# Order of the first loads and casts, zero matmuls ahead of the hash products, and GpSimd output splits in the last pair of an LSH attention with two MLPs

## The chip, the cores and the metric

The kernel runs on one core of a Trainium2 chip. The time is the device time of one execution in microseconds (us); of several executions the median counts. The engines are TensorE (matmuls and transposes), VectorE, ScalarE, GpSimd and SyncE; rows of the profile call them PE (and PEld for its weight loads), DVE, ACT, POOL and SP. Each runs its own instructions in the order of the program and waits at semaphores for the others. DMA transfers are issued by SyncE, ScalarE or GpSimd.

## The reference

Attention within hash buckets, and then two MLPs on the result:

```python
def _attn_ref(q, k, v, proj):                  # q, k, v: (2, 8, 768, 64); proj: (64, 6)
    q_bits = (np.einsum('bhsd,dk->bhsk', q, proj) > 0).astype(np.int64)
    k_bits = (np.einsum('bhsd,dk->bhsk', k, proj) > 0).astype(np.int64)
    powers = 2 ** np.arange(n_bits)
    q_bucket = np.sum(q_bits * powers, axis=-1)
    k_bucket = np.sum(k_bits * powers, axis=-1)
    mask = q_bucket[:, :, :, None] == k_bucket[:, :, None, :]
    scores = scale * np.matmul(q, k.transpose(0, 1, 3, 2))
    scores = np.where(mask, scores, -1000000000.0)
    scores = scores - np.max(scores, axis=-1, keepdims=True)
    attn = np.exp(scores)
    attn = attn / (np.sum(attn, axis=-1, keepdims=True) + 1e-09)
    return np.matmul(attn, v)

def _moe_ref(x, w_gate, w_val, w_out):         # x: (1536, 512), inner width 1536
    gate = 1.0 / (1.0 + np.exp(-(x @ w_gate)))
    return gate * (x @ w_val) @ w_out

def _moe2_ref(x, w_in, w_out):                 # inner width 2048
    h = x @ w_in
    g = np.where(h >= 1, h, np.where(h <= -1, 0.0, (h + 1) ** 2 / 4))
    return g @ w_out
```

The three weights of the first MLP and the two of the second come as 64-bit floats; the attention's tensors are 32-bit.

## The kernel before

**Attention.** Heads are worked in eight pairs, four for each of the two batches. A pair is 12 units: a head (two) times a block of 128 queries (six). For a unit, `QK` makes 128x768 scores with eight or fewer matmuls in two banks, `MAX` (VectorE, line 304) the negated row maximum, `EXP` (ScalarE, line 308) the exponentials P and their row sums. `Flip` turns P: `T` transposes it on TensorE into a pt tile (two buffers, line 330), `HI` (ScalarE, line 339) and `LO` (VectorE, line 342) write its high and low half in 16 bits into PT. The products with v (`pv`, line 381) add up in a tile O; `evac` (VectorE, line 388) multiplies it by the reciprocal row sums and writes the attention output xr. The reciprocals are spread over 64 columns by GpSimd (`rb`, line 316), transposed on TensorE (r, line 499) and copied by ScalarE (rs).

**Operands.** All matmuls that need 32-bit accuracy work on a high half and a low remainder. `Prep` makes them for q and k of a pair: U is the high half and W the remainder; in a second role, H and N hold the one-hot rows of the hash buckets beside a head's values, so that the mask is part of the product. Two heads lie in the upper and lower 64 partitions, so halves have to be moved between partitions by DMA (line 274; for the first pair `first_moves`, line 245, which fills B, N and H from U, and `swap`, line 258, which writes W's half over the U half that was moved away). The hash: `z` (line 218) multiplies U and W by the projection in pz, `bits` (ScalarE, line 221) takes signs into bt, `xp` (line 227) multiplies bt by the code table, and `Hot` and `Hot_k` (lines 232 and 261) turn that into one-hot rows.

For the first pair U is made by ScalarE and W by VectorE (`UW`, lines 199 and 200); for the later pairs both by GpSimd (`scale`, `top`, `rest`). v is scaled by its largest magnitude and split by GpSimd (`split_v`: the reduction vm on VectorE, a row vrow through two small DMAs, then three GpSimd steps).

**MLPs.** The attention output is split the same way: `split` makes the high half on ScalarE (line 140) and the remainder on VectorE (line 141), four tiles x_0 to x_3 for each batch. `gv` makes the first chunk of gate and value products for batch 0 in two halves of 24 matmuls, still among the attention's work; a program-wide loop over further chunks, `out1` and `mlp2` follow. The 64-bit weights are brought to 32 bits with ScalarE and VectorE steps (`conv_w`, lines 94 to 104); those of the first chunk are made during the first pair by a generator `first_weights`, called as `fw`.

**The order.** All of attention is written under a manual schedule: engines run what the program says in that order. The start (`constants`, loads, hash of pair 0) is written out by hand. After it each step has a due time in units, from the table `AT` or a number beside `at(...)`; the steps are sorted by due time, and this is the order on each engine. `UP` is 12, so a pair's steps are 12 later than those of the pair ahead of it. SyncE's DMAs stand in the same order in one queue. The attention outputs of batch 0 are split at 1.5, 4.5, 7.5 and 10.5 of the last pair, those of batch 1 from 13 on, and `gv(0)` stands at 12.6.

## Time and profile before

| | us |
|---|---|
| median of three runs | 841.71 (840.47 to 841.99) |
| profiled execution | 837.76 |
| its span, first to last instruction | 836.0 |

| engine | busy us of the span | instructions |
|---|---|---|
| PE | 802.6 (96%) | 5072 |
| PEld | 734.8 (88%) | 5072 |
| DVE | 557.4 (67%) | 982 |
| ACT | 461.9 (55%) | 877 |
| POOL | 102.3 (12%) | 92 |

TensorE is busy through nearly all of the span, so the whole is read by stretches: the first 44 us fill the pipeline, the pairs in the middle run back to back, the last pair and the first gate products lie between 216 and 272 us, and the MLPs follow to the end. In the profile's 40 slices of 20.9 us, TensorE shows 3 tenths in the first slice, 7 in the second, 8 in the twelfth and thirteenth, 7 in the last, and else 9.

### The profile page before, as it was taken

How to read it: one execution, taken by the hardware profiler on the slowest of the kernel's cores; microseconds unless marked ns; L12 is line 12 of the kernel's file. 1: busy time of each engine (PE TensorE's matmuls, PEld its weight loads, DVE VectorE, ACT ScalarE, POOL GpSimd, SP SyncE). 2: the span in 40 equal slices, each digit the busy share in tenths (PEclk: the TensorE clock that was granted, in tenths of full speed). 3: DMA queues.
4: the chain of work that ended last, by engine and by line, in shares of the span. 5: the costliest groups of instructions: out<-in, count | busy, mean ns of one | idle time of the engine just before them, and what ended most of it. 6: DMA issues, size and time to landing. Idle time of an engine off the chain costs nothing.

```text
span 836.0 us, 13001 instructions
## 1 busy us (share of the span) xinstructions
PE 802.6 (96%) x5072; PEld 734.8 (88%) x5072; DVE 557.4 (67%) x982; ACT 461.9 (55%) x877; POOL 102.3 (12%) x92
## 2 busy tenths in 40 slices
PE   3799999999988999999999999999999999999997
PEld 2688888888766999999999999999989898989996
DVE  5898889889984845434588777999943435444443
ACT  3788888888874423222333345557654555555453
POOL 5254345435020000000000000000000000000000
PEclk9899999999999999999999999999999999999999
DMA  7444443453200521221146330543300001000001
GB/s 210 109 100 114 124 113 89 114 141 69 58 1 1 183 70 51 82 70 51 51 156 188 110 102 0 176 152 118 111 1 1 0 1 76 1 1 1 0 1 77
DMA packets 39486, 64.22 MB, mean 77 GB/s; under 512 B 5220, under 2 KB 27876, under 8 KB 39424
## 3 DMA queue, kind: packets, MB, share of 16 engines
q1 hardware_dynamic: 39168, 63.20, 26.0%
q8 instruction: 40, 0.66, 0.3%
q14 instruction: 22, 0.18, 0.1%
q0 software_dynamic: 112, 0.12, 0.1%
q10 hardware_dynamic: 144, 0.07, 0.0%
HBM read 45.27 MB, written 3.15 MB: 58 GB/s over the span
## 4 chain that ended last, share of the span: by engine, by line
PE 87%; DVE 6%; ACT 3%; DMA 2%; issue 1%; POOL 0%; DVEq 0%; ACTq 0%; SPq 0%; POOLq 0%
PE sc L296 7%; PE pt L330 7%; PE O L381 6%; PE p L127 5%; PE p L129 5%; PE p L128 5%; PE o L654 5%; PE o L655 5%; PE o L653 5%; PE pg L129 4%; PE pv L129 4%; PE pg L127 4%; PE pv L127 4%; PE pv L128 4%; PE pg L128 4%; PE y L127 3%
## 5 line engine op out<-in xcount | busy, mean ns | idle before, releaser
L342 DVE SCALAR_TENSOR_TENSOR PT<-pt,PT 128x512 f16<-128x512 f32 x144 | 96.2, 684 | 10.0 <-ACT PT L339 6.8
L339 ACT ACTIVATE PT<-pt 128x512 f16<-128x512 f32 x144 | 82.3, 597 | 24.9 <-PE pt L330 23.9
L304 DVE TENSOR_REDUCE st<-sc 128x1 f32<-128x768 f32 x96 | 90.7, 946 | 7.4 <-PE sc L296 7.4
L308 ACT ACTIVATE P<-sc,st 128x768 f32<-128x768 f32 x96 | 86.8, 904 | 11.6 <-DVE st L304 11.5
L330 PE MATMUL pt<-ident,P 128*128 128x128 f32 x576 | 83.5, 279 | 7.0 <-DVE PT L342 6.2
L127 PE MATMUL p<-yh,wh_i 128*128 128x384 f32 x256 | 86.0, 336 | 0.2 <-DVE yl L610 0.2
L129 PE MATMUL p<-yh,wl_i 128*128 128x384 f32 x256 | 85.9, 336 | 0.0
L128 PE MATMUL p<-yl,wh_i 128*128 128x384 f32 x256 | 85.7, 335 | 0.0
L330 PEld LDWEIGHTS pt<-ident,P 128*128 128x128 f32 x576 | 66.2, 142 | 21.4 <-DVE PT L342 15.0
L655 PE MATMUL o<-wh_o,gl 128*128 128x512 f32 x192 | 75.3, 392 | 0.0
L654 PE MATMUL o<-wl_o,gh 128*128 128x512 f32 x192 | 75.2, 392 | 0.0
L653 PE MATMUL o<-wh_o,gh 128*128 128x512 f32 x192 | 74.7, 389 | 0.0
L637 DVE SCALAR_TENSOR_TENSOR g<-p,t 128x384 f32<-128x384 f32 x64 | 35.4, 553 | 48.3 <-ACT t L635 48.3
L153 DVE SCALAR_TENSOR_TENSOR h<-sg,pv 128x384 f32<-128x384 f32 x48 | 26.4, 550 | 56.0 <-PE pv L129 56.0
L151 ACT ACTIVATE sg<-pg 128x384 f32<-128x384 f32 x48 | 23.4, 487 | 66.1 <-PE pg L129 65.8
L381 PE MATMUL O<-PT,vh 128*64 128x256 f16 x576 | 54.9, 278 | 2.6 <-DVE xr L388 2.6
L634 ACT ACTIVATE t<-p,cst 128x384 f32<-128x384 f32 x64 | 36.6, 572 | 36.8 <-PE p L129 36.8
L638 ACT ACTIVATE gh<-g 128x384 fp32r<-128x384 f32 x64 | 33.6, 525 | 41.8 <-DVE g L637 41.7
L639 DVE TENSOR_TENSOR gl<-g,gh 128x384 fp32r<-128x384 f32 x64 | 35.7, 557 | 31.5 <-ACT gh L638 31.5
L127 PEld LDWEIGHTS p<-yh,wh_i 128*128 128x128 f32 x256 | 48.1, 188 | 1.6 <-DVE yl L610 0.5
L128 PEld LDWEIGHTS p<-yl,wh_i 128*128 128x128 f32 x256 | 48.1, 188 | 1.1
L117 DVE TENSOR_TENSOR wl_o<-w_o,wh_o 128x512 fp32r<-128x512 f32 x56 | 38.5, 688 | 14.6 <-ACT wh_o L116 14.6
(256 smaller groups left out, 2009.9 us busy)
## 6 DMA issues: line engine op xcount, KB each, us to landing
wr_o<-in_moe_w_out_dram SPq DMA_DIRECT2D x28, 512.0 KB, 3.5
wr_i<-in_moe_w_in_dram SPq DMA_DIRECT2D x16, 512.0 KB, 3.8
wr_g<-in_moe_w_gate_dram SPq DMA_DIRECT2D x12, 512.0 KB, 3.8
wr_v<-in_moe_w_val_dram SPq DMA_DIRECT2D x12, 512.0 KB, 4.2
n<-in_qt_dram SPq DMA_DIRECT2D x8, 384.0 KB, 3.5
n<-in_kt_dram SPq DMA_DIRECT2D x8, 384.0 KB, 3.9
U<-W SPq DMA_DIRECT2D x16, 192.0 KB, 2.5
vr<-in_v_dram SPq DMA_DIRECT2D x8, 384.0 KB, 3.6
```

What stands on the lines that cost most here:

```text
L127: nc.tensor.matmul(ps, lhsT=wh, rhs=rh, start=first, stop=False)
L128: nc.tensor.matmul(ps, lhsT=wh, rhs=rl, start=False, stop=False)
L129: nc.tensor.matmul(ps, lhsT=wl, rhs=rh, start=False, stop=last)
L304: nc.vector.tensor_reduce(out=self.st[:, 0, self.c:self.c + 1], in_=self.sc[:, :, 0:HN], op=ALU.max, axis=AX.XY, negate=True)
L308: nc.scalar.activation(out=self.P, in_=self.sc[:, :, 0:HN], func=AF.Exp, bias=self.st[:, 0, self.c:self.c + 1], scale=1.0, accum_out=self. ...
L330: nc.tensor.transpose(self.ps[m][:, j, :], un[2 * self.n + e].P[:, a, c:c + 128], ident)
L339: nc.scalar.activation(out=self.part(0, m), in_=self.ps[m], func=AF.Copy, scale=PSCALE)
L342: nc.vector.scalar_tensor_tensor(out=self.part(1, m), in0=self.ps[m], scalar=PSCALE, in1=self.part(0, m), op0=ALU.mult, op1=ALU.subtract)
L381: nc.tensor.matmul(O_ps[r, 0:GN], lhsT=vv[m][:, e, i * D:(i + 1) * D], rhs=PT[:, l, e * NI + i, :], start=(s == 0), stop=(s == len(steps) ...
L653: nc.tensor.matmul(oacc[i], lhsT=gh[:, ts], rhs=wh, start=(fc == 0), stop=False)
L654: nc.tensor.matmul(oacc[i], lhsT=gh[:, ts], rhs=wl, start=False, stop=False)
L655: nc.tensor.matmul(oacc[i], lhsT=gl[:, ts], rhs=wh, start=False, stop=(fc == F2 - 1))
```

## The change

Five things are changed.

1. The projection's two loads are issued by ScalarE ahead of ident, where GpSimd issued them; the code table's load is GpSimd's first instruction, where it was the last of its constants. bt is zeroed by VectorE, ahead of pz.
2. The code table is cast by VectorE right behind pz, where the cast stood behind the B casts of the first pair. The first step of `first_weights` (ScalarE's w_abs) moves behind the one-hot rows of pair 0.
3. Twelve matmuls of bt by itself, when bt is all zeros, stand ahead of the hash products; they write a score bank that nothing reads.
4. For the first pair, the vm reduction of v and the four small steps on vrow stand later. For all others, the copies N<-U of the next pair are due right behind the GpSimd cast that makes U, and some due times of GpSimd steps have other numbers. The rb copy is a step of its own with the same due time.
5. `split_x` is made of two GpSimd instructions; batch 0's stand at 5.0, 6.7, 8.4 and 10.1 of the last pair, three of batch 1's behind the last reciprocals. The last split of batch 1 stays with ScalarE and VectorE and moves ahead of the second half of `gv`.

```diff
     def constants():
+        nc.scalar.dma_start(proj_sb[E], proj)
+        nc.scalar.dma_start(proj_sb[O], proj)
+        nc.gpsimd.dma_start(code_f, code_d)
+        nc.scalar.dma_start(ident, ident_d)
+        nc.vector.memset(bt, 0.0)
         nc.vector.memset(pz.bitcast(F32), 0.0)
         nc.gpsimd.memset(code, 0.0)
-        nc.gpsimd.memset(bt, 0.0)
...
-        nc.scalar.dma_start(ident, ident_d)
-        nc.gpsimd.dma_start(proj_sb[E], proj)
-        nc.gpsimd.dma_start(proj_sb[O], proj)
-        nc.gpsimd.dma_start(code_f, code_d)
...
+        nc.vector.tensor_copy(code[0:ZR], code_f)
...
             load_qk(*seq[1], nc.sync)
+            idle = sc_tile("idle")
+            for i in range(12):
+                nc.tensor.matmul(idle[:, 0, 0:HN], lhsT=bt[:, 0:128], rhs=bt, start=True, stop=True)
...
-            next(fw)
             p1.scale()
...
-            nc.vector.tensor_copy(code[0:ZR], code_f)
             pp.bits()
...
             pp.done()
+            next(fw)
...
+                "TOP": (-3.20, -1.20),
+                "RST": (-2.90, -0.90),
...
             def split_x(b, c):
-                X[b, c] = split(X[b, c], f"x{b}_{c}", qtile)
+                src, hi, lo = X[b, c], qtile(f"x{b}_{c}h"), qtile(f"x{b}_{c}l")
+                nc.gpsimd.tensor_copy(out=hi, in_=src)
+                nc.gpsimd.tensor_tensor(out=lo, in0=src, in1=f(hi), op=ALU.subtract)
+                X[b, c] = hi, lo
...
-                at("VR", 0, q - 1, split_v, b, p, 0)
-                at("VT", 0, q - 1, split_v, b, p, 1)
-                for h, d in ((2, 1.65), (3, 2.65), (4, 4.65)):
+                vs = [AT["VR"][0] - UP, AT["VT"][0] - UP, AT["V2"][0], AT["V3"][0], AT["V4"][0]]
+                if q == 0:
+                    vs[:2] = AT["MAX"][1] + 0.001, AT["MAX"][2] + 0.3
...
-                    at(-0.7 if q else -0.9, 0, q, on, q + 1, "copy", 0, 0)
-                    at(-0.65, 0, q, on, q + 1, "copy", 1, 0)
+                    at(AT["TOP"][0] + 0.001 if q else -0.9, 0, q, on, q + 1, "copy", 0, 0)
+                    at(AT["TOP"][1] + 0.001 if q else -0.65, 0, q, on, q + 1, "copy", 1, 0)
...
             for c in range(KC):
-                at(1.5 + 3 * c, 0, last, split_x, 0, c)
+                at(5.0 + 1.7 * c, 0, last, split_x, 0, c)
             for c in range(KC - 1):
-                at(UP + 1.0 + 0.7 * c, 0, last, split_x, 1, c)
-            at(UP + 0.6, 0, last, gv, 0)
+                at(AT["ST"][2] + 0.1 + 0.01 * c, 0, last, split_x, 1, c)
+            at(AT["T"][17] + 0.5, 0, last, gv, 0)
             for d, o, fn, args in sorted(prog, key=lambda x: x[:2]):
                 fn(*args)
+            X[1, KC - 1] = split(X[1, KC - 1], f"x1_{KC - 1}", qtile)
             gv(1)
-            split_x(1, KC - 1)
```

VectorE at the start of the program, before: W are the remainders of pair 0's q and k, B their moved copies, code the cast table, H and N one-hot rows, vm the reduction of v, st a row maximum.

```order
L200 SCALAR_TENSOR_TENSOR W_0_0_102<-n_0_0_76,U_0_0_101 128x768
L200 SCALAR_TENSOR_TENSOR W_0_0_106<-n_0_0_78,U_0_0_105 128x768
L253 CAST B_119<-W_0_0_102 64x768
L253 CAST B_123<-W_0_0_106 64x768
L450 CAST code<-code_f 56x512
L261 TENSOR_SCALAR H_0_0_107<-xp_0_0_162 64x768
L261 TENSOR_SCALAR N_0_0_108<-xp_0_0_162 64x768
L350 TENSOR_REDUCE vm_0_174<-vr_0_153 128x1
L304 TENSOR_REDUCE st_0_0_0_178<-sc_0_0_0_169 128x1
```

The cast of the table stands behind W and B, and vm ahead of the first maximum. The same place now (its line numbers are one higher, or one lower for vm):

```order
L75 CAST code<-code_f 56x512
L201 SCALAR_TENSOR_TENSOR W_0_0_116<-n_0_0_76,U_0_0_115 128x768
L201 SCALAR_TENSOR_TENSOR W_0_0_120<-n_0_0_78,U_0_0_119 128x768
L254 CAST B_133<-W_0_0_116 64x768
L254 CAST B_137<-W_0_0_120 64x768
L262 TENSOR_SCALAR H_0_0_121<-xp_0_0_173 64x768
L262 TENSOR_SCALAR N_0_0_122<-xp_0_0_173 64x768
L305 TENSOR_REDUCE st_0_0_0_187<-sc_0_0_0_182 128x1
L98 TENSOR_SCALAR w_g_180<-w_g_180 128x512
L99 TENSOR_SCALAR w_g_180<-w_g_180 128x512
L305 TENSOR_REDUCE st_0_0_0_187<-sc_0_1_0_189 128x1
L349 TENSOR_REDUCE vm_0_201<-vr_0_165 128x1
```

The cast has moved ahead of W, and vm behind the second maximum.

VectorE in the last pair, before, around the second split of batch 0 (PT is line 342's output, x_1l the split's remainder, xr the attention output that `evac` writes):

```order
L304 TENSOR_REDUCE st_3_0_2_3286<-sc_3_0_3_3329 128x1
L141 TENSOR_TENSOR x_1l<-xr_1_935,x_1h 128x768
L388 SCALAR_TENSOR_TENSOR xr_2_3115<-O_2_2_3251,rs_2_1_5_3291 128x256
L342 SCALAR_TENSOR_TENSOR PT_3_0_3248<-pt_2_3351,PT_3_0_3248 128x4x128
L342 SCALAR_TENSOR_TENSOR PT_3_1_3377<-pt_0_3365,PT_3_1_3377 128x4x128
```

One row of a split stands among the rows of the pair. The same place now:

```order
L305 TENSOR_REDUCE st_3_0_2_3295<-sc_3_0_3_3338 128x1
L387 SCALAR_TENSOR_TENSOR xr_2_3128<-O_2_2_3264,rs_2_1_5_3300 128x256
L341 SCALAR_TENSOR_TENSOR PT_3_0_3261<-pt_2_3360,PT_3_0_3261 128x4x128
L341 SCALAR_TENSOR_TENSOR PT_3_1_3386<-pt_0_3370,PT_3_1_3386 128x4x128
L305 TENSOR_REDUCE st_3_0_2_3295<-sc_3_1_3_3381 128x1
```

The row x_1l is gone and nothing else has moved.

GpSimd in the last pair, before, from the three steps on v (vr, vh, vl) to the end, with the three rb copies:

```order
L362 TENSOR_SCALAR vr_3_3008<-vr_3_3008,vm_3_3143 128x768
L365 CAST vh_3_3278<-vr_3_3008 128x768
L316 COPY rb_3_1_1_3284<-st_3_0_0_3150 128x256
L369 TENSOR_TENSOR vl_3_3363<-vr_3_3008,vh_3_3278 128x768
L316 COPY rb_3_1_3_3459<-st_3_0_2_3286 128x256
L316 COPY rb_3_1_5_3557<-st_3_0_4_3419 128x256
```

Nothing stands between the rb copies there but vl. Now, from vl on:

```order
L368 TENSOR_TENSOR vl_3_3368<-vr_3_3021,vh_3_3287 128x768
L529 CAST x_0h<-xr_0_510 128x768
L530 TENSOR_TENSOR x_0l<-xr_0_510,x_0h 128x768
L529 CAST x_1h<-xr_1_949 128x768
L530 TENSOR_TENSOR x_1l<-xr_1_949,x_1h 128x768
L525 COPY rb_3_1_3_3468<-st_3_0_2_3295 128x256
L529 CAST x_2h<-xr_2_1388 128x768
L530 TENSOR_TENSOR x_2l<-xr_2_1388,x_2h 128x768
L529 CAST x_3h<-xr_3_1827 128x768
L530 TENSOR_TENSOR x_3l<-xr_3_1827,x_3h 128x768
L525 COPY rb_3_1_5_3570<-st_3_0_4_3428 128x256
L529 CAST x_0h<-xr_0_2266 128x768
```

Each rb copy after the first stands behind two splits of batch 0, and batch 1's splits follow the last one.

## Rows read from the trace of the kernel before

**Rows 1.** View by stretches: stretch, busy PE, PEld, DVE, ACT, POOL; clock, DMA, GB/s

```profile
16.00:24.00 8.00, 6.42 (x21) 5.36 (x20) 7.13 (x13) 3.69 (x6) 1.81 (x2) 0.57 0.50 157
...
44.00:224.00 180.00, 178.75 (x1576) 149.02 (x1576) 161.21 (x278) 152.66 (x315) 79.28 (x68) 1.00 0.42 104
224.00:257.00 33.00, 27.42 (x251) 21.50 (x248) 28.30 (x48) 24.82 (x51) 6.61 (x7) 1.00 0.01 1
```

**Rows 2.** Chain that ended last, first 20 us: start, length, what

```profile
2.32 6.18 DMA proj_sb<-in_proj_dram
...
8.92 2.47 DVE W L200 x2
...
13.38 1.95 DVE code L450
...
17.79 1.66 PE sc L296 x4
```

**Rows 3.** Instructions of line 245, SyncE queue: issue ns, first and last start

```profile
L245 SPq DMA_DIRECT2D B<-U x2: 539/570/600, 5.5 to 7.0; - x2
```

**Rows 4.** The same for line 258, the swap

```profile
L258 SPq DMA_DIRECT2D U<-W x2: 461/462/462, 12.6 to 13.5; - x2
```

**Rows 5.** DMA issues: count, size each, median us from issue to landing

```profile
U<-W SPq DMA_DIRECT2D x16, 192.0 KB, 2.5
...
B<-U SPq DMA_DIRECT2D x2, 192.0 KB, 6.7
...
code_f<-in_code_dram POOLq DMA_DIRECT2D x1, 112.0 KB, 8.8
ident<-in_ident_dram ACTq DMA_DIRECT2D x1, 64.0 KB, 4.1
```

**Rows 6.** Timeline of VectorE, 18 to 28 us: start, length, [idle before it]

```profile
18.11 0.93 DVE L350 TENSOR_REDUCE vm<-vr 128x1 f32<-128x768 f32 x1
...
27.22 0.69 DVE L418 TENSOR_TENSOR wl_g<-w_g,wh_g 128x512 fp32r<-128x512 f32 x1 [1.28 <-ACT wh_g L415]
```

**Rows 7.** Groups by shape, VectorE, 223 to 257 us: busy, mean ns, idle before

```profile
L141 DVE TENSOR_TENSOR x_2l<-xr,x_2h 128x768 fp32r<-128x768 f32 x1 | 1.0, 959 | 0.9 <-ACT x_2h L140 0.9
L141 DVE TENSOR_TENSOR x_3l<-xr,x_3h 128x768 fp32r<-128x768 f32 x1 | 1.0, 959 | 1.1 <-ACT x_3h L140 1.1
L141 DVE TENSOR_TENSOR x_0l<-xr,x_0h 128x768 fp32r<-128x768 f32 x1 | 1.0, 957 | 1.0 <-ACT x_0h L140 1.0
L141 DVE TENSOR_TENSOR x_1l<-xr,x_1h 128x768 fp32r<-128x768 f32 x1 | 0.9, 946 | 0.0
```

**Rows 8.** Waits of TensorE, 216 to 257 us: total, times, longest

```profile
PE pt L330 <- DVE PT L342: 3.1, 5, 1.1
PE r L499 <- POOL vh L365: 1.6, 1, 1.6
```

**Rows 9.** Timeline of TensorE in the last pair

```profile
240.75 0.66 PE L330 MATMUL pt<-ident,P 128*128 128x128 f32 x4 [0.92 <-DVE PT L342]
```

**Rows 10.** Waits of TensorE, 257 to 272 us

```profile
PE O L381 <- DVE xr L388: 2.6, 1, 2.6
```

**Rows 11.** Groups of GpSimd, 44 to 216 us

```profile
L209 POOL TENSOR_TENSOR W<-n,U 128x768 fp32r<-128x768 f32 x12 | 21.9, 1821 | 0.5
...
L206 POOL CAST U<-n 128x768 fp32r<-128x768 f32 x12 | 9.9, 824 | 0.4
```

**Rows 12.** Timeline of GpSimd in the last pair

```profile
234.09 1.65 POOL L369 TENSOR_TENSOR vl<-vr,vh 128x768 f16<-128x768 f32 x1
247.21 0.40 POOL L316 COPY rb<-st 128x256 f32<-128x256 f32 x1 [11.47 <-DVE st L314]
```

**Rows 13.** All of line 342 on VectorE: ns min/median/max

```profile
L342 DVE SCALAR_TENSOR_TENSOR PT<-pt,PT x144: 659/682/693, 29.7 to 262.3; 128x512 f16<-128x512 f32 x144
```

**Rows 14.** Line 97 on VectorE, two executions, 18 to 40 us

```profile
L97 DVE TENSOR_SCALAR w_g<-w_g x1: 417/417/417, 20.3 to 20.3; 128x512 f32<-128x512 f32 x1
L97 DVE TENSOR_SCALAR w_v<-w_v x1: 1045/1045/1045, 27.8 to 27.8; 128x512 f32<-128x512 f32 x1
```

More of the change, by code (lines that the diff above doesn't have):

```diff
@@ L549, in lsh_attention_glu_act @@
                     if q:
[L550 to L552 removed]
+                        at(min(AT["SCL"][0], AT["TOP"][0], AT["TOP"][1]) - 0.01, 0, q, prep, q + 1)
+                        at("SCL", 0, q, on, q + 1, "scale")
+                        for j in range(2):
+                            at("TOP", j, q, on, q + 1, "top", j)
+                            at("RST", j, q, on, q + 1, "rest", j)
                     for i in range(4):
```

32 lines of the change are left out of this document (20 added, 12 removed).

## The prediction

> **What bounds the kernel now.** I read the busy time by stretches first. From 44 to 224 us TensorE works 178.75 of 180 us, so nothing that the change moves there can be worth much. Between 16 and 24 us it is busy at a mean granted clock of 0.57, while VectorE is busy 7.13 of 8 us; and from 224 to 257 us, the last pair of heads, TensorE works only 27.42 of 33 us [rows 1]. The change touches the two loose places: the first 24 us and the last pair.
>
> Second, the chain of the first 20 us. It runs through one engine: the projection's DMA (6.18 us of chain, up to 8.50), the two W residuals (2.47), the two B casts, the cast of the code table (13.38 to 15.33), the code products, the one-hot rows, and the first scores at 17.79, which take 1.66 us [rows 2]. Third, what stands next to this chain: the B moves issued at 5.5 and 7.0 us [rows 3] land 6.7 us later, behind the loads ahead of them in SyncE's queue [rows 5]. The swaps that must wait for them go out at 12.6 and 13.5 [rows 4] and land 2.5 us later [rows 5]. So the last swapped U is there at about 16.1, and scores can't end before that, however early the chain is.
>
> Fourth, the last pair. VectorE makes the low halves of four attention outputs there: about 0.95 us each, three of them after 0.9 to 1.1 us of standing still for ScalarE's high half [rows 7]. That is 3.8 us of work and 3.0 of idling, 6.8 us in all, on the engine that TensorE waits for: 3.1 us in five waits for line 342, and 1.6 us ahead of one r [rows 8]. The last row names GpSimd's vh, but r reads an rb made long before; what it lacks is a pt bank, which line 342 frees, and line 342 stood behind x_0l.
>
> **The change, part by part.** *Projection loads.* They go from third place in GpSimd's program to first in ScalarE's queue, issued at about 0.7 us. The nearest row is ident, issued there at that time before: 4.1 us [rows 5]. So proj is there at about 5, not 8.5. The costs on ScalarE are two more issues ahead of its table load; the first U waits for q anyway.
>
> *The code table.* Its load becomes the first of GpSimd's queue, some 2 us earlier, and its cast moves from behind the B casts to ahead of the W residuals. Everything on VectorE is then queued behind that load. Bounds for its flight: ident's 4.1 us (half the bytes) and its own 8.8, third in the queue [rows 5]; so it lands between 4.8 and 9.5. I take 7, between the two, since two thirds of the time were spent with two loads ahead of it. The cast costs between 0.6 us (two thirds of a B cast) and the 1.95 of the chain [rows 2]; I take 0.7. Then W at 7.7 to 10, not 8.92 to 11.38, and the 2 us of cast between B and the code products are gone: scores could begin near 13.7, 4 us early.
> [...]
>
> *What is late next.* The swap. Its bound does not move: the loads ahead of the B moves are the same. The first unit's last score matmuls then run at 16.1 instead of 18.6, and end near 17.0 instead of 19.45: 2.4 us, not 4.
>
> *The vm reduction* stood at 18.11 in VectorE's wait for the first scores, at no cost; it now stands behind the second row maximum, in a stretch in which VectorE never rests: plus 0.93 us. Some returns, since VectorE idles 1.28 us ahead of wl_g [rows 6]: the reduction eats that idle, but half a microsecond of it also belongs to ScalarE, whose work comes earlier with the maxima. I charge 0.5. **Start: 2.4 - 0.5 = 1.9 us.** Ends: minus 0.5 (late table) to 3.1.
>
> *Twelve matmuls on zeros* (384 columns each) use TensorE from about 1 to 5 us, when it has nothing else: no cost. At the lower of the two levels the first scores took 1.66 us for four, so each matmul some 0.4; at the upper one half of that. The gain is the clock, if it holds. Before, TensorE stood still for most of 13 to 17.8 us and then worked at 0.5; now the hash products come earlier, but the wait for the swap (to 16.1) remains. I take nothing, and 1.2 us as the upper end (half of 1.66, and as much as 0.4 later in the first pair).
>
> *Smaller moves*, at nothing. The w_g absolute value on ScalarE moves behind the one-hot rows: it needs to be there only by VectorE's clamp, after the first maximum. SyncE now issues N<-U ahead of vrow<-vm in seven pairs; vrow then waits for GpSimd's cast of U, which VectorE's vm comes after. If that cover went, the v scale would be late by as much as the cast, 0.82 us at most [rows 11]. GpSimd's own order in pairs 2 to 7 is unchanged, and TensorE's order has no other change.
>
> *The output splits.* Four leave ScalarE and VectorE in the last pair, and three more in the drain. The wait of 1.6 us ahead of r goes; so do 0.92 at 240.75, behind x_1l [rows 9], and the 1.1 behind x_2l [rows 8]; what stands behind x_3l is shorter, since the products are next. Of the 4.7 us of both rows I take 4.0; the rest are waits with no split ahead. Ends: 1.6 (the one wait that certainly sits behind a split) and 5.4 (4.7, and 0.7 of smaller waits). **Last pair: 4.0 us.**
> On GpSimd a split is a cast and a subtraction of 128x768, 0.82 + 1.82 = 2.65 us [rows 11]. The four of batch 0 begin when vl is done, at 235.7; two fit before the rb copy at 247.2 that stands between them, two after it take till 252.6 [rows 12], and the gate products need the last at about 258. All of this shifts to earlier times together. Cover: some 5 us.
>
> *The drain.* TensorE waits 2.6 us for the evacuation of the last O but one [rows 10]. Ahead of that evacuation VectorE now has no x_0l of batch 1: minus 0.95 us, the length of its four like [rows 7]; I take 0.9, ends 0 and 1.0. The x_3 split of batch 1 moves ahead of the second gate product; its result is needed after, at nothing.
>
> **The sum.** 1.9 + 4.0 + 0.9 = 6.8 us. The profiled execution took 837.76 us (span 836.0, 1.76 around it), so it would take 831.0. The median of the three runs shown is 841.71, 3.95 above it; the difference carries over, and the forecast is 841.71 - 6.8 = **834.9 us**.
>
> **Rivals.**
> *Late table.* If code_f takes 8.8 us from its early issue, it lands at 9.5; GpSimd is then at work, the cast takes 2 us, W ends at 14.1 (not 11.38), the swap goes out at 14.9 and the first scores end where they did. With the vm reduction the start loses 0.5: 841.71 + 0.5 - 4.9 = 837.3. For it: the load shares full queues. Against it: two loads fewer ahead. 0.15.
> *The waits move.* In the last pair another wait follows each one that is taken away (VectorE is still busy 24 of 33 us), and only the 1.6 us come: 841.71 - (1.9 + 1.6 + 0.9) = 837.3. Against it: from 44 to 224 us VectorE is 161.21 of 180 us busy, denser than that, and TensorE hardly waits [rows 1]. 0.13.
> *The clock holds* from the zeros into the first pair: 1.2 more, 833.7. 0.08.
> *GpSimd slows VectorE* (the other side). Line 97 took 1045 ns beside GpSimd's scaling of v and 417 without [rows 14]. If line 342 and the row maxima suffered so, each by 0.6 us, some 14 of them in the 10.6 us of the four splits would cost 8.8 us on the engine that paces the pair: 841.71 - 6.8 + 8.8 = 843.7. It decides from 0.5 us each. Against it: line 342 ran 144 times, many beside GpSimd, within 659 to 693 ns [rows 13]. 0.05.
> [...]
> *It does not do what it says*: the zeros change no clock and the splits were in slack, which leaves under 1.7 us. 0.04.
>
> **How the numbers follow.** The forecast has 0.55. The range reaches from the upper ends (3.1 + 5.4 + 0.9 = 9.4, so 832.3) to two unfavourable cases at once (minus 0.5, 1.6 and 0.9: 2.0, so 839.7); what is left out is the slowed VectorE and half of the last rival, with some for the unforeseen. 0.2%, 1.7 us, is about what a measurement of this kernel can tell from no change. Faster: forecast, late table, moved waits and held clock, 0.91, less 0.03 where two meet: 0.88. Same 0.06, slower 0.06.
>
> **What would show it.** The W residuals should begin near 7.7 us, the first scores end near 17.0, TensorE be at the same instruction some 2 us earlier at 44 us and unchanged in pace to 224; the last pair should hold under 2 us of TensorE waits, with line 342 at 680 ns; the wait for the evacuation should be near 1.7. The prediction is wrong if the cast of the code ends after 9.5, if swaps go out at other times than 12.6 and 13.5, if line 342 takes more than 0.7 us beside a split, or if the gate products wait for GpSimd.

## The result: 830.25 us, 11.4 us less

The changed kernel takes 830.25 us (median of 4 runs, 829.85 to 831.45); the kernel before beside it took 841.64 (4 runs, 840.47 to 841.99). The ratio is 0.9869, interval 0.9852 to 0.9887. The forecast was 834.9 with a range from 832.3: the direction was right, the time lies 2 us below the range.

The two profiled executions are closer together than the medians: 837.76 and 829.85, 7.9 us, against 6.8 in the sum. The distance between an execution and the median is the thread of what follows: the median that the forecast started from lay 3.95 us above the kernel before's profiled execution; the changed kernel's lies 0.4 above its own.

**Where the 7.9 us of the two traces lie.** The r transposes stand in the same order on TensorE in both kernels, so their start times tell how far the program has come (those of the last pair are counted by time, from 222 us on):

| r transposes | before | after | difference |
|---|---|---|---|
| first | 40.38 | 38.53 | -1.85 |
| eighth | 107.61 | 105.15 | -2.46 |
| of the start of the last pair | 221.61 | 219.46 | -2.15 |
| third of the last pair | 252.75 | 246.25 | -6.50 |
| last, in the drain | 265.09 | 257.01 | -8.08 |
| end of the span | 836.0 | 827.8 | -8.2 |

So 1.85 us come from the start, 0.3 net from the middle, 4.35 up to the third r of the last pair and 1.6 behind it, 0.9 of these being the shorter wait for the evacuation. (The spans differ by 8.2 us, 0.3 more than the executions.)

One pair of traces is a thin base for the first of these terms. In the nine traces of this study with the start of the kernel before, the first r stands anywhere from 39.29 to 41.75 us, median 40.38; in the seven with the changed start, with or without zeros, from 38.16 to 39.64, median 38.55. The medians differ by 1.83 us, so the term holds, but a difference of 1 us in the first r of two single traces says nothing.

The stretches that answer to [rows 1] (stretch, busy time of PE, PEld, DVE, ACT, POOL; granted clock, DMA share, GB/s):

```profile
16.00:24.00 8.00, 7.59 (x33) 6.63 (x34) 6.40 (x13) 2.85 (x6) 1.67 (x1) 0.69 0.52 156
42.00:222.00 180.00, 178.95 (x1582) 149.17 (x1580) 161.78 (x278) 153.40 (x315) 79.70 (x68) 1.00 0.42 104
222.00:255.00 33.00, 31.09 (x276) 25.80 (x270) 26.34 (x46) 23.57 (x49) 23.28 (x20) 1.00 0.01 1
```

TensorE works 31.09 of 33 us in the last pair, where it worked 27.42, and GpSimd 23.28 where it worked 6.61.

The chain of the first 20 us of the changed kernel (start, length, what), against [rows 2]:

```profile
1.17 4.42 DMA n<-in_kt_dram
...
5.62 0.85 ACT U L200
...
7.00 6.36 DMA B<-U
...
13.51 2.77 DMA U<-W
...
16.41 0.99 PE sc L297 x2
...
17.43 0.96 DVE st L305
```

The chain no longer runs through VectorE. It runs through K's load, U, the B move of 6.36 us and the swap, as the prediction said of "what is late next". Line 259's swaps go out when those of [rows 4] did, and the loads have these flights (count, KB each, median us to landing):

```profile
L259 SPq DMA_DIRECT2D U<-W x2: 461/462/462, 12.7 to 13.5; - x2
```

```profile
B<-U SPq DMA_DIRECT2D x2, 192.0 KB, 6.8
code_f<-in_code_dram POOLq DMA_DIRECT2D x1, 112.0 KB, 5.4
ident<-in_ident_dram ACTq DMA_DIRECT2D x1, 64.0 KB, 5.9
proj_sb<-in_proj_dram ACTq DMA_DIRECT2D x2, 1.5 KB, 4.7
```

On VectorE the second half of the projection came last, at 6.91, not the code table, whose cast took 0.42 us (start, length, what, [idle before it]):

```profile
6.91 0.17 DVE L73 CAST pz<-proj_sb 64x6 fp32r<-64x6 f32 x1 [1.90 <-DMA proj_sb<-in_proj_dram]
7.11 0.16 DVE L74 TENSOR_TENSOR pz<-proj_sb,pz 64x6 fp32r<-64x6 f32 x1
7.30 0.42 DVE L75 CAST code<-code_f 56x512 bf16<-56x512 f32 x1
7.65 1.81 DVE L201 SCALAR_TENSOR_TENSOR W<-n,U 128x768 fp32r<-128x768 f32 x2
```

The waits of TensorE in the last pair (214 to 255 us) and in the drain, against [rows 8] and [rows 10] (total, times, longest), and all of line 341, which is line 342 of [rows 13]:

```profile
PE pt L329 <- DVE PT L341: 0.5, 2, 0.3
PE sc L297 <- ACT P L309: 0.4, 1, 0.4
PE sc L297 <- DMA H<-U: 0.4, 1, 0.4
PE r L507 <- DVE PT L341: 0.4, 1, 0.4
```

```profile
PE O L380 <- DVE xr L387: 1.7, 1, 1.7
```

```profile
L341 DVE SCALAR_TENSOR_TENSOR PT<-pt,PT x144: 660/690/693, 27.2 to 255.1; 128x512 f16<-128x512 f32 x144
```

The five waits of 3.1 us and the one of 1.6 are down to two of 0.3 at most, and VectorE's low halves have kept their pace beside GpSimd's splits. One line is new: TensorE waits 0.4 us for the DMA H<-U. The prediction did not speak of that copy; waits for it turned out to be a part of the missing microseconds.

### The profile page after: what moved, and what is told of

Same layout as the page of the kernel before. It is cut to its first block, busy times and chain, and to the rows that moved or that the text cites. A ratio compares the mean times of both kernels' runs of the same rounds, so it can differ in the third digit from the quotient of the medians.

```text
span 827.8 us, 13043 instructions
## 1 busy us (share of the span) xinstructions
PE 805.3 (97%) x5084; PEld 735.8 (89%) x5084; DVE 550.4 (66%) x976; ACT 457.3 (55%) x870; POOL 117.8 (14%) x103
## 4 chain that ended last, share of the span: by engine, by line
PE 80%; DVE 10%; DMA 6%; ACT 2%; issue 2%; SPq 0%; DVEq 0%; ACTq 0%
PE sc L297 7%; PE pt L329 7%; PE O L380 6%; PE o L676 5%; PE o L677 5%; PE o L675 5%; PE p L128 4%; PE p L130 4%; PE p L129 4%; PE pg L130 4%; PE pv L129 4%; PE pv L130 4%; PE pg L128 4%; PE pv L128 4%; PE pg L129 4%; PE y L129 2%
## 5 line engine op out<-in xcount | busy, mean ns | idle before, releaser
L309 ACT ACTIVATE P<-sc,st 128x768 f32<-128x768 f32 x96 | 86.9, 905 | 13.5 <-DVE st L305 13.2
```

Source lines behind the costliest of these rows:

```text
L309: nc.scalar.activation(out=self.P, in_=self.sc[:, :, 0:HN], func=AF.Exp, bias=self.st[:, 0, self.c:self.c + 1], scale=1.0, accum_out=self. ...
```

## First experiments: the parts apart

**The kernel before again**, unaltered, for the spread of its executions.

> The kernel before, unchanged. Its profiled execution took 837.76 us and its other executions 840.5 to 842.0; the changed kernel has no such distance (829.85 profiled, 829.85 to 831.45). Theory A: the 3.9 us are spread over the whole span (slower DMA or clock everywhere), and a profiled execution of about 841 us is later by a little in every stretch. Theory B: the kernel has two courses at its start, and an execution of 841 us is already 3 to 4 us late when TensorE becomes the bound at about 44 us (r at 43 to 44 us, not 40.4). Theory C: the distance arises in the last pair or the drain, so r is at 40.4 as before and the first gate products at 261, not 257.3.

Measured: 840.27 (12 runs, 838.92 to 844.95), beside 23 runs of the same kernel at 840.41 (836.05 to 843.25). One kernel's executions lie up to 8.9 us apart. Its trace, of 839.62 us, waits at two places in the middle of the attention, 1.0 us near 76 us and 1.2 near 106, where the first trace had waited 0.3 at each. None of the three theories holds as it stands, though C names the drain: the first r is 1.1 us earlier than in the first trace, and 2.9 us are lost behind it, 1.6 in the middle and 1.4 behind the last pair's third r, where the granted clock is 0.80 over 262 to 266 us and 0.77 over 266 to 270 (1.00 in the first trace).

**The changed kernel without the matmuls on zeros.**

```
-            for i in range(12):
-                nc.tensor.matmul(idle[:, 0, 0:HN], lhsT=bt[:, 0:128], rhs=bt, start=True, stop=True)
```

> The changed kernel without the twelve matmuls on zeros; all else as changed. If they are worth nothing, as forecast, 830.3 us, and the first scores end at 17.4 us with or without them. If they keep TensorE's clock up in the first pair, 831 to 833. If they are what removes the 3.3 us of distance between the profiled and the other executions (theory B with the clock as its cause), 833.5.

Measured: 832.05 (5 runs), ratio 0.9901 (0.9875 to 0.9928), so 1.8 us more than the changed kernel's 830.25 and 1.4 more than its repetition below. These medians are of different sessions and the intervals of the ratios overlap (0.9852 to 0.9887 and 0.9854 to 0.9902), so the loss rests on the trace more than on the times. The trace showed two losses: the first r only 0.75 us earlier than before's (the changed kernel's 1.85), and the waits of the middle were there again:

```profile
PE sc L297 <- DMA H<-U: 1.8, 2, 1.2
```

The first seemed to be the clock (0.67 in 30 to 42 us, the changed kernel 0.95). A later run corrects this.

**The kernel before with the splits alone** (GpSimd's seven splits, their places, and the last split ahead of the second gate product).

```
-                X[b, c] = split(X[b, c], f"x{b}_{c}", qtile)
+                src, hi, lo = X[b, c], qtile(f"x{b}_{c}h"), qtile(f"x{b}_{c}l")
+                nc.gpsimd.tensor_copy(out=hi, in_=src)
+                nc.gpsimd.tensor_tensor(out=lo, in0=src, in1=f(hi), op=ALU.subtract)
...
-                at(1.5 + 3 * c, 0, last, split_x, 0, c)
+                at(5.0 + 1.7 * c, 0, last, split_x, 0, c)
...
```

> The kernel before with the output splits of the changed one alone (seven on GpSimd, their places, the last split ahead of the second half of gv). From the trace of after, the last pair and the drain are 5.9 us shorter. Theories A and B: 841.6 - 5.9 = 835.7 us. Theory C (the long executions of before lose 3.3 us more in the last pair, and this is what goes): 832.4. The forecast's own terms gave 4.9, so 836.7.

Measured: 832.95 (6 runs), ratio 0.9915 (0.9890 to 0.9939): 7.5 us, where the prediction's two terms make 4.9. The 7.5 us lie between the 5.9 of theories A and B and the 9.2 of C and decide for neither. The trace shows 5.9 us from the last pair's start to the last r, and 2.0 us lost again from there to the end (572.9 us, before 570.9): TensorE's granted clock falls behind the drain's wait for the evacuation, which ends at 259.86 (0.90 and 0.68 in these stretches).

```profile
258.00:262.00 4.00, 2.26 (x27) 1.69 (x28) 1.49 (x3) 0.38 (x1) 1.35 (x1) 0.90 0.02 4
262.00:266.00 4.00, 4.00 (x27) 3.47 (x24) 1.33 (x2) 0.84 (x1) 0.00 (x0) 0.68 0.00 0
```

**The changed kernel with before's splits** (the start, the zeros and the reordered SyncE queue alone).

> The changed kernel with the output splits of the kernel before: loads, casts, zeros and due times as changed. From the trace of after, the start is 1.9 us and the middle 0.3 to 0.6 us shorter. Theory A or C: 841.6 - 2.3 = 839.3 us. Theory B (the start of before has a long course, which the change removes): 836.0.

Measured: 837.75 (12 runs), ratio 0.9964 (0.9947 to 0.9981): 2.7 us, and the first r again 1.83 us earlier. Theories A and C had 2.3 us and B 5.6, so B is out: the start has no long course that the change removes. With the 7.5 us of the splits it makes some 10 us, as much as the changed kernel gains in the repetition below (840.86 to 830.62). Its trace showed something else. TensorE stands still 1.55 us ahead of the last pair's first r, as in [rows 8], and then runs for most of 4 us at the lower of the two levels of the clock that these traces show (0.50 and 1.00); the kernel before, in its first trace, stood still as long and went on at 1.00. Stretches of this run, 0.57 being the granted clock:

```profile
222.00:232.00 10.00, 7.75 (x72) 6.20 (x71) 7.93 (x15) 7.51 (x15) 3.77 (x2) 1.00 0.01 2
232.00:236.00 4.00, 3.90 (x22) 2.81 (x22) 2.19 (x5) 1.86 (x4) 2.01 (x2) 0.57 0.00 0
236.00:250.00 14.00, 11.75 (x104) 9.30 (x104) 12.15 (x19) 10.41 (x21) 0.40 (x1) 1.00 0.01 1
```

Between the last pair's first and second r it lost 1.5 us on the kernel before. The clock falls a second time in the drain, to 0.57 over 266 to 270 us.

**A theory for the middle.** Each pair's one-hot rows go through four copies on SyncE's queue, with a load between them: N<-H and H<-U for queries, the load of the next V, then N<-H and H<-U for keys. The next pair's first scores need the last of them, and start as it lands. In the repeated kernel before, ahead of the fourth pair (SyncE's queue: issue time, length of the issue, what):

```profile
94.31 0.47 SPq L274 DMA_DIRECT2D N<-H  x1
98.53 0.46 SPq L274 DMA_DIRECT2D H<-U  x1
99.04 0.59 SPq L171 DMA_DIRECT2D vr<-in_v_dram  x1
100.04 0.46 SPq L274 DMA_DIRECT2D N<-H  x1
103.60 0.46 SPq L274 DMA_DIRECT2D H<-U  x1
```

The first N<-H takes 4.2 us instead of 2.5. H<-U must wait for it, V's load for H<-U, and so that load (384 KB) goes out 1.0 us ahead of the second N<-H, which then takes 3.6; the scores come 1.2 us late. Why the first copy is slow stands in the DMA view of those 4.2 us (busy share of the 16 engines in 40 slices, in tenths; then queues and the flight):

```profile
DMA  0000000009577969588200000010010010000000
...
q1 hardware_dynamic: 80, 0.20, 21.4%
q8 instruction: 1, 0.02, 2.7%
...
N<-H SPq DMA_DIRECT2D x1, 192.0 KB, 4.2
```

One packet of the instruction queue falls into the copy. It took 2.7% of 16 engines over 4.2 us, so 1.8 us of one engine. The bulk of the copy is over by slice 21, 2.2 us after the issue; three single slices follow, up to 1.3 us later, as packets would come that stood behind it on one engine; that is my reading and is not shown, as these rows do not tell the engine. A copy without such a packet, in a later run, has no such tail and takes 2.5 us:

```profile
DMA  0000000000000019959959779420000000000000
...
q1 hardware_dynamic: 80, 0.20, 27.9%
...
N<-H SPq DMA_DIRECT2D x1, 192.0 KB, 2.5
```

By its landing the first copy took 4.2 us, though its bulk was over after 2.2, and H<-U went out only then. The 18 traces of this study bear the packets out: each has seven rounds of these copies, 126 in all, and in 59 a packet of the instruction queue begins between 0.2 us ahead of the first N<-H's issue and 2.2 us behind it. These 59 copies take 2.55 to 4.46 us, the other 67 all 2.49 to 2.58.

Where the packets fall can be moved. By the trace's records of single packets they lie some 14.4 us apart, two to a pair of 28.5 us, and TensorE runs some 253 instructions in that time (1582 + 1580 in the 180 us from 42 to 222 us of the changed kernel). Over the whole span of that trace 40 packets of this queue (0.66 MB, so some 16 KB each) stand against 10168 instructions of TensorE (5084 matmuls, 5084 weight loads), 254 to a packet. By an estimate from these counts, if the packets come with TensorE's instructions, the 24 (12 matmuls, 12 weight loads) that the zeros add move each packet by 24/254 of 14.4, 1.4 us. The traces agree in the direction and roughly in the size: against the first N<-H of the first four rounds of copies (those for the second to the fifth pair; the expectations below count these rounds as pairs 1 to 7) the packet stood at +0.5, +1.0, +0.9 and +2.5 us before, and at -1.7, -0.6, -0.05 and +0.6 after; without the zeros alone it stood at +0.3, +1.0, +1.15 and +2.7, 1.2 to 2.2 us later than with them.

The zeros do not rid the kernel of these packets but move them: from the fourth round on they fall into the first copies of the changed kernel (+0.5 to +1.1 us). Ahead of the last pair TensorE waits 0.36 us for that, and in the kernel with before's splits, with the same zeros, 1.55 us: a packet at +1.6, a first copy of 4.2 us and a second of 3.75.

## Second experiments: V's load, and the packets' place

**The changed kernel again.**

> The changed kernel unaltered, for its own spread. Theory A (a 16 KB packet of the instruction queue that falls into the first copy N<-H of a pair holds that copy, behind it the load of V, the second N<-H, H<-U and the next pair's first scores): TensorE's wait ahead of a pair's first scores is 0 to 0.5 us at six pair starts and 0.3 to 1.0 at the seventh (the copy issued near 206.5), the last pair holds no stretch under 0.9 of the clock between 222 and 270 us, and the executions spread by under 3 us (829.5 to 832.5). Rival B (the distances between executions are the same for every kernel): they spread by 5 us or more, as those of the kernel before do (836.0 to 843.3).

Measured: 830.62 (5 runs, 829.44 to 832.44), a spread of 3.0 us. The trace waits 0.3 us at the last pair only, behind a first N<-H of 3.5 us with an instruction packet in it, and its clock is 1.00 from 42 us on.

**V's load early in the changed kernel.**

```
-                    at(5.9, 0, q, load_v, *seq[q + 1])
+                    at(2.5, 0, q, load_v, *seq[q + 1])
```

> The changed kernel with each pair's load of V due at 2.5 instead of 5.9, so that it goes out behind the loads of Q and K and no longer right ahead of the second N<-H. Theory A: the second N<-H takes 2.5 to 2.6 us at all seven pairs, TensorE waits 0 for H<-U, the pairs after start every 28.5 us, and the time is 0.3 to 0.6 us under that of the changed kernel beside it (about 829.8 where that has 830.2). Rival: V's load isn't what holds the second copy, and the seventh pair still waits 0.3 us or more.

Measured: 829.32 (828.88 to 831.0). All seven second copies take 2.5 to 2.6 us, although first copies of 3.3, 3.3 and 4.1 us are among them, and no wait is left in the middle. The time is 1.3 us under the run beside it, more than the trace's 0.3; with spreads of 2 to 3 us that excess is not shown.

**The same without the zeros.**

> The changed kernel without the 12 matmuls on zeros, and with V's load due at 2.5. Without them alone the time was 832.05, with waits of 0.7 and 1.2 us ahead of the third and fourth pair. Theory A (those waits are the instruction packets' phase, which the 12 matmuls shift): the waits are gone and the time is 830.3 to 831.0; what is left against the changed kernel is the start's 0.8 to 1.1 us. Rival C (the zeros act through the clock of the first 40 us alone): the time stays at 831.5 to 832.5. In both the clock's row for 30 to 42 us stays below that of the changed kernel (0.67 against 0.95).

Measured: 829.8 (828.73 to 830.09). The two waits are gone and rival C is out; theory A had them go, but by this run it is V's early load that takes them away. I was wrong on the start: the first r stands 1.97 us earlier than before's, as in the changed kernel, and the clock of 30 to 42 us is 0.97. So the slow start of the first run without zeros was that execution's, not the zeros'; the run with zeros and V early had a first r as late (39.64 us, and 39.63 there), at a clock of 0.92. The zeros give the start nothing that these runs can show. What they gave in the change is the packets' place.

**Twice the instructions on zeros**, for the same columns.

```
-            for i in range(12):
-                nc.tensor.matmul(idle[:, 0, 0:HN], lhsT=bt[:, 0:128], rhs=bt, start=True, stop=True)
+            for i in range(24):
+                nc.tensor.matmul(idle[:, 0, 0:HN // 2], lhsT=bt[:, 0:128], rhs=bt[:, 0:HN // 2], start=True, stop=True)
```

> The changed kernel with 24 matmuls on zeros of 192 columns for its 12 of 384: the same columns, twice the instructions. Theory A (the instruction packets come by instruction count): all packets of the first 220 us lie some 3 to 4 us earlier against the copies than in the changed kernel (-1.7 us against the first N<-H of pair 1 there, -5 here), the seventh pair's wait is gone, and the time is 829.5 to 830.3. Rival D (only TensorE's time and clock matter): the packets lie where they did, and the time is that of the changed kernel within 0.3 us.

Measured: 829.38 (828.84 to 830.73). The last pair's wait is gone: all 14 copies take 2.5 to 2.6 us, none with a packet in it. The packets did move earlier, but by 0.1 to 1.6 us in the second to fourth round, not by 3 to 4; only in the first was it more (6.6 us ahead of the copy instead of 1.7). That the number of instructions places the packets holds; my size for it was too large, and the estimate of 1.4 us above is nearer.

## Third experiments: single terms

**V's load early in the kernel before.**

> The kernel before with one edit, each pair's load of V due at 2.5 instead of 5.9. Theory A: the waits ahead of the third and fourth pair (0.3 and 0.3 us in one execution of the kernel before, 1.0 and 1.2 in another) are gone, the second N<-H takes 2.5 to 2.6 us at all pairs, and the time is 0.6 to 2.2 us under that of the kernel before (838.2 to 839.8 where that has 840.4). Rival: those waits are not what sets the distance between executions, and the time stays within 0.4 us.

Measured: 838.79 (12 runs, 835.57 to 840.18), ratio 0.9962 (0.9947 to 0.9976): 2.9 us under the 841.64 beside it. No wait is left between 42 and 222 us, with a first copy of 4.2 us among the seven. That is more than the 0.6 to 2.2 us of the two traces, by less than the scatter of single executions.

**Batch 0's splits alone in the kernel before.**

```
+                if b:
+                    X[b, c] = split(X[b, c], f"x{b}_{c}", qtile)
+                    return
...
-                at(1.5 + 3 * c, 0, last, split_x, 0, c)
+                at(5.0 + 1.7 * c, 0, last, split_x, 0, c)
```

> The kernel before with the four splits of batch 0 alone on GpSimd, at the changed kernel's places; batch 1's splits, the drain and the start stay. It measures the term of the last pair by itself. Theory E (the prediction's 4.0 us was too small because the wait of 1.55 us ahead of r also lets TensorE's clock fall in some executions, to 0.57 over 232 to 236 us in one, worth 1.5 us): no stretch of the last pair below 0.9 of the clock up to 250 us, the last r transposes 4.2 to 5.0 us earlier against those of 221 us than in the kernel before, and a time of 834.6 to 836.0 where that has 840.4. Rival F (the waits alone): 4.0 us, 836.4 or above.

Measured: 834.43 (6 runs, 833.85 to 836.72), ratio 0.9919 (0.9901 to 0.9937): 7.2 us. In the trace the last pair is 4.4 us shorter up to the third r and 4.8 up to the last, with a clock of 1.00 up to 250 us. So the prediction's 4.0 us stand against 4.8 in this trace, and 2.4 us more of the median are not in it; the median fell more than either theory gave (4.0, and 4.4 to 5.8). From the last r to the end the trace then loses 1.8 us (572.7, before 570.9), at a mean clock of 0.91 over 250 to 270 us.

**The cast of the code table back behind the B casts**, in the changed kernel.

```
-        nc.vector.tensor_copy(code[0:ZR], code_f)
...
+            nc.vector.tensor_copy(code[0:ZR], code_f)
             pp.bits()
```

> The changed kernel with the cast of the code table back behind the B casts; its load and the projection's stay early. The prediction's step (the swaps end the start, whatever VectorE does ahead of them): swaps go out at 12.6 and 13.5 as before, the scores that need them start near 16.4, the second r transposes stand where the changed kernel's do within 0.4 us if the clock of 12 to 42 us is alike, and the time is that of the changed kernel, 830.2, within 0.8. Rival G (the earlier cast carries the start's gain): first scores and the time 1.5 to 2.0 us later, 832 or above.

Measured: 830.47 (5 runs). VectorE of this run:

```profile
6.85 1.83 DVE L200 SCALAR_TENSOR_TENSOR W<-n,U 128x768 fp32r<-128x768 f32 x2
8.71 1.14 DVE L253 CAST B<-W 64x768 fp32r<-64x768 f32 x2
9.78 0.41 DVE L450 CAST code<-code_f 56x512 bf16<-56x512 f32 x1
```

The table is ready at 10.2, before the code products want it, in either place. The one-hot rows are done 0.7 us earlier than with the cast first, and it helps nothing, because the swaps bound the start. The B moves flew 7.3 us in this run (6.8 in the changed kernel's), the second swap waited for them to 14.1 instead of 13.5, the scores came at 16.98 instead of 16.4, and the first r stands 0.6 us later, within the scatter of the changed start. So G is out, and the cast's place is worth nothing that this run shows once the loads are early.

**The gate weights' load behind the swaps**, with V early.

```
             load_qk(*seq[0], nc.sync)
             constants()
-            load_w(w_gate, "g")
...
                 pp.swap(j)
+            load_w(w_gate, "g")
             load_v(*seq[0], nc.sync)
```

> The changed kernel with V's loads due at 2.5 and with the first gate weights (512 KB) loaded behind the swaps instead of ahead of the B moves. If the B moves' flight of 6.4 us behind that load sets the swaps: they go out at 11.3 to 11.8 instead of 12.67 and 13.5, the scores that need them start at 14.4 to 15.2 instead of 16.4, and the time is 0.8 to 1.5 us under that of the changed kernel with V's loads early (829.3). Rival H (the gain is taken by the next wait: the weights' first step on ScalarE stands ahead of the first exponentials, or V's load is late for its maximum): the first scores are earlier, and the second r transposes and the time are not, 829.0 or above.

Measured: 827.65 (5 runs, 826.81 to 829.76), ratio 0.9844 (0.9821 to 0.9866), below the changed kernel's 830.25 and 830.62. SyncE's swaps, and TensorE's first scores:

```profile
L259 SPq DMA_DIRECT2D U<-W x2: 461/461/461, 10.4 to 11.9; - x2
```

```profile
14.40 0.62 PE L297 MATMUL sc<-H,H 128*128 128x384 f32 x2 [1.52 <-ACT N L233]
14.86 0.51 PE L297 MATMUL sc<-U,U 128*128 128x384 f32 x2
15.21 0.51 PE L297 MATMUL sc<-N,N 128*128 128x384 f32 x2
```

With 512 KB less ahead of the B moves the swaps go out at 10.4 and 11.9, 2.3 and 1.6 us earlier (the first of them earlier than I had written, the second 0.1 later), and the scores no longer wait for them but for ScalarE's one-hot rows, at 14.40. In the changed kernel that same row stands at 14.29, and is followed by 1.11 us of waiting:

```profile
14.29 1.01 PE L297 MATMUL sc<-H,H 128*128 128x384 f32 x2 [1.58 <-ACT N L233]
16.41 0.98 PE L297 MATMUL sc<-U,U 128*128 128x384 f32 x2 [1.11 <-DMA U<-W]
```

The first r stands at 37.53 us, 2.85 earlier than before's and 1.0 earlier than the changed kernel's, ahead of all seven traces with the changed start. This is the fastest kernel of the study. It has two edits; beside the changed kernel with V early alone (829.32, ratio 0.9871, 0.9846 to 0.9896) the later load is 1.7 us of median, in another session and with intervals that overlap, so its size rests on the trace. Rival H may have a part in it: the gate weights now land at 16.3, ScalarE's first step on them waits 1.99 us and stands ahead of the first exponentials. Whether that costs anything was not run.

## Fourth experiments: what the kernel before's usual execution is made of

Two single edits of the kernel before took 2.9 and 7.2 us off its median, both more than their traces showed. Four kernels, with neither, either and both, were to tell whether they add.

> The kernel before with both single edits, V's loads due at 2.5 and batch 0's four splits on GpSimd. Alone they gave 2.9 us (838.79 for 841.64) and 7.2 us (834.43), though the trace of the second shows only 4.8 us less in the last pair. Theory J (the 2.4 us above the trace are the last pair's own, by the clock): both add to 10 us, about 831.3 where the kernel before has 841.4. Theory K (that excess is a matter of executions with and without the waits ahead of the third and fourth pair, which V's early load takes away too): both give 7.5 to 8.2 us, 833.2 to 834.0, with a spread of under 2 us.

> The kernel before with V's loads due at 2.5, once more, beside the others on one chip: 2 to 3 us under the kernel before. Its trace is a further look at the last pair: with the wait of 1.55 us ahead of r, the clock of 232 to 236 us is at 1.00 or near 0.57 (1.5 us more).

> The kernel before with batch 0's splits on GpSimd, once more: 834.4 by its earlier runs (7.2 us under the kernel before), 836.0 to 836.6 by its trace (4.8 to 5.4 us). Theory J: 7 us again with waits of 0.5 to 2.5 us at the third and fourth pair in its trace. Theory K: 5 to 6 us, or waits under 0.5 us in a trace of 834.5 or less.

> The kernel before, unaltered, for another trace and more times: a median of 840 to 842. If its usual distance to the profiled 837.76 is made of the waits at the third and fourth pair and of stretches at half the clock in the last pair or the drain, a trace at 840 or above shows 1.0 us or more of the former above the 0.56 us of the first trace, or a mean clock under 0.95 in 222 to 270 us; a rival, that the distance lies in the gated MLP behind the attention, would show that stretch 2 us or more longer than 570.8 us.

Measured, on one chip, beside 23 runs of the kernel before at 841.14 (837.09 to 845.15):

| kernel | median us | ratio, interval |
|---|---|---|
| before, again | 839.57 (12 runs) | 0.9982, 0.9966 to 0.9998 |
| V early | 837.83 (12 runs) | 0.9967, 0.9951 to 0.9983 |
| batch 0's splits | 834.67 (6 runs) | 0.9924, 0.9898 to 0.9949 |
| both | 833.94 (6 runs) | 0.9917, 0.9890 to 0.9943 |

The first row says how far to trust the others: the same kernel lies 1.6 us apart from itself, at an interval that leaves 1 out. By the medians the edits do not add: 3.3 and 6.5 us alone, 7.2 together, at the time that theory K gave and 2.6 us above theory J's. That is not clear of the noise: the product of the two single ratios, 0.9891, lies just inside the interval of both. And K is not clean either. The spread of both is 3.2 us, and the trace of batch 0's splits, at 837.24 its slowest run, waits 2.8 us at two pair starts, while its median lies only 0.7 above the kernel that never waits there. How often an execution of each kernel waits is not known; a trace shows one.

The third trace of the kernel before is the useful one. It took 841.92 us, a usual time for this kernel, with a span 4.1 us longer than the first trace's, and the r transposes say where: 1.0 us in the start; 1.3 ahead of the third and fourth pair (waits of 1.6 and 0.2 where the first trace had 0.3 and 0.3); 1.4 between the first and second r of the last pair; 0.45 behind the last r, so the MLPs are not where the distance lies. The 1.4 is the clock again (stretches of this run):

```profile
222.00:236.00 14.00, 11.63 (x103) 9.14 (x101) 12.52 (x25) 10.11 (x21) 4.09 (x3) 1.00 0.02 2
236.00:240.00 4.00, 4.00 (x26) 3.33 (x24) 2.38 (x3) 1.76 (x4) 2.01 (x2) 0.57 0.00 0
240.00:250.00 10.00, 8.59 (x77) 6.71 (x75) 8.14 (x12) 8.72 (x18) 0.00 (x0) 1.00 0.01 2
```

Of six traces with the wait of 1.55 us ahead of the last pair's first r, two show such a stretch behind it; of twelve with batch 0's splits on GpSimd, none between 222 and 250 us. The repeated trace with V early shows the other side: after the same 1.55 us its clock stays at 1.00.

The drain shows the same more often. The mean granted clock of 250 to 270 us is 1.00 in twelve of the 18 traces, 0.91 in five (the first repetition of the kernel before, the splits alone, the changed kernel with before's splits, and both traces with batch 0's splits alone) and 0.83 in the one with both edits:

```profile
250.00:270.00 20.00, 16.67 (x104) 14.59 (x103) 7.40 (x12) 6.24 (x10) 0.00 (x0) 0.83 0.02 3
```

All six falls begin between 0.6 us ahead of the end of TensorE's wait for the evacuation and 1.6 us behind it, as the two in the last pair begin within 1.6 us behind the end of the wait ahead of r. No other falls between 42 and 820 us in any of the traces. By the length of the drain's wait: with 2.6 us, as before, five traces of nine show the fall; with 1.7, as changed, one of nine. Where it comes in a kernel with batch 0's splits alone or with the splits alone, the way from the last r to the end takes 572.4 to 572.9 us; in the kernels with a clock of 1.00 there it takes 569.2 to 571.3. So some of what the splits gain in the last pair is lost again in these traces.

The middle is clearer. From the first r to the r of the last pair's start the six traces with V early take 180.6 to 180.7 us, whatever else they have, and the one with 24 zeros too. With V late and without zeros, seven traces take 181.2 to 183.4, and the lowest of them is the first trace of the kernel before. With 12 zeros and V late, four take 180.9, 180.9, 181.1 and 182.1. No trace with V early, and none with the zeros, waits more than 0.4 us at the third or fourth pair.

## Why the prediction was too small

*Projection, code table, swap.* Right, and in size: W begins at 7.65 (7.7 said), the swaps go out at 12.7 and 13.5 (12.6 and 13.5), the scores that need the swap start at 16.41 (16.1). The start gives 1.85 us (1.9). That the swap is what is late next is shown twice, by the cast put back (nothing lost) and by the swaps made earlier (1.0 us more). W's start was hit by two errors that cancel: the table was there at 6.7 (5.4 us of flight) and its cast took 0.42 us (7 and 0.7 said), but the second half of the projection came last, at 6.88 and not at about 5. The scores of the first unit ended at 17.39, not 17.0, at a clock of 0.69.

*Zeros.* "I take nothing" was right of the clock in the start. That they move the instruction packets of 220 us of program I had not thought of; leaving them out brings back waits of 1.8 us in a trace.

*Last pair.* 4.0 us said, 5.0 measured in the traces (4.35 up to the third r and 0.7 of the rest behind it, without the evacuation); the kernel with batch 0's splits alone shows 4.8. The mechanism was the one named: the waits of [rows 8] went, GpSimd was done in time, line 341 kept 690 ns. Of the 4.7 us of those two rows 0.5 are left, and some 0.8 more went that stand in no listed wait. The end of 5.4 holds it.

*Drain.* 0.9 said; TensorE's wait fell from 2.6 to 1.7. That the clock falls behind the longer wait in five traces of nine, and behind the shorter in one, the prediction did not have.

*The sum* of 6.8 is so 1.1 us short of the 7.9 of the profiled executions, nearly all of it in the last pair.

*The step that failed* is the last: "the difference carries over". The 3.95 us from the profiled 837.76 to the median were taken as a thing outside the change, in the forecast and in both ends of the range. But the changed kernel's median lies 0.4 us above its trace: 3.55 of the 4.65 us between forecast and result went with the change. What the runs show in place of a fixed distance are waits for the copies and stretches at half the clock, which the first trace of the kernel before by luck hardly had and which its two other traces have: its middle took 181.2 us, where the median of six traces with that middle is 182.7 and that of four with the changed one 181.0; and its clock falls behind neither wait. The row that told of it was there: [rows 1] has 1.25 us of idle TensorE in 44 to 224 us, half of it two waits at pair starts, which I passed over as too small to matter. The waits are shown to come from the copies, and to go with V's early load or with other places of the packets. The clock's fall is shown to come at the end of TensorE's standstills in the last pair and the drain, in eight cases; that the standstill is its cause, and why it comes in one execution and not in the next, is not shown. By an estimate from these traces the waits make some 1.3 us of the 3.55, the falls in the last pair 0.5 (1.5 us in two of six) and those in the drain 0.8 (some 1.7 us in five of nine against one of nine). With so few traces, and with single edits whose medians move more than their traces, the shares and the rest stay open.

*Rivals.* "The clock holds" (833.7) had the sign of what happened, in the wrong place: I looked for it in the first pair, and the stretches at half the clock that the change takes away lie in the last pair and the drain. The others did not come.

## What to carry to other kernels

A profile is one execution. Where medians lie several microseconds above it, take a second and a third trace of the same kernel before a forecast, and ask what each differs in; the difference is not a constant that survives the change. A chain of copies that ends just as its reader starts (here 5.1 us of copies for every pair) has no wait in one trace and a microsecond in the next: look at who else uses the queue right ahead of it, and move a load that has time. And shortening a wait of TensorE may give back more than its length, where the clock falls behind it in some executions: look at the granted clock behind every wait of more than a microsecond, in several traces, and not only where you look for the gain.

## What was not expected of the hardware

One 16 KB packet of instructions in a copy of 192 KB lengthens its flight from 2.5 us (2.49 to 2.58 in the 67 copies without one) to as much as 4.5 (2.55 to 4.46 in the 59 with one). Twelve matmuls at the start of a program moved these packets against the copies of the whole attention, and with them waits of 1.8 us in a trace. And TensorE's clock fell for most of 4 us (0.57) after it had stood still 1.55 us, in two traces of six with the same instructions there, and after it had stood still 2.6 us in five of nine.
